# Talking-heads attention with a Fourier feed-forward: the output kept in SBUF, or summed in DRAM by adding DMAs

## The chip, the core and the metric

The kernel runs on one core of one Trainium2 chip. The metric is device time in microseconds (us); before the change it is 2406.89 us, the median of four runs (2404.97 to 2409.32). All data are float32. The program is written with a tile framework: pools hand out buffers ("tiles"), and the framework places the semaphore waits.

## The reference, cut to what matters

```python
# q, k, v: (8, 12, 448, 64); attention gives x: (8, 448, 768)
X = np.fft.fft(np.fft.fft(x, axis=1), axis=2)
u = x + np.real(X)
un = (u - mean(u)) / np.sqrt(var(u) + 1e-06)      # over the last axis
ch = np.maximum(un @ w_ch1, 0.0) @ w_ch2           # 768 -> 3072 -> 768
return u + ch
```

The attention mixes its twelve heads with 12x12 matrices before and after the softmax. What matters here is the last line: the result is u plus the feed-forward's output.

## The kernel before, in words

The first third of the time (to about 860 us) is attention and the Fourier mix; it leaves u in DRAM scratch. The rest is `ffn_phase`, and the change lies there alone.

**Tiles and loops.** The 3584 rows of u are cut into NTB = 7 row tiles of 512, the 3072 hidden columns into NC = 6 chunks of 512. The loop of L1079 runs over n = 0 to 41, with c, t = divmod(n, 7): all seven row tiles with chunk 0, then all seven with chunk 1, and so on. One such step is called a block here. A block calls `first(n)` (un times a chunk of w_ch1, then ReLU, the matmuls of L980) and `second(n, h)` (the result times a chunk of w_ch2, the matmuls of L1036). Both are done in a Strassen-Winograd form: seven products i in the order of L837 (0, 4, 5, 1, 6, 2, 3), on three PSUM accumulators named P, Q and R (L839). An accumulator is read after a product and goes on accumulating the next one.

**The output.** `second` makes 128x384 results, two (x = 0, 1) for each product. After each, VectorE adds the accumulator to a piece of u in SBUF (L1042): products 0 and 1 go to the quarter (0, 0) of the row tile's output, 4 and 6 to (1, 1), 5 and 2 to (0, 1), and 3 to (1, 0). So u itself becomes the output, chunk by chunk, and all seven u tiles (12 KB a partition each) stay in SBUF through all six chunks; in the last chunk SyncE's queue stores each finished piece (L1045, 56 stores). Three u tiles lie in one pool (L856), the other four in a pool opened after block 0 (L1092), when the mixing phase's memory is returned.

**What else runs in a block.** In chunk 0 the next row tile is normed and transposed (`stats`, `power`, `norm`, `turn`, `total`), its transposed pieces are stored to DRAM (L963), and u of the tile after next is loaded (`load_u`, L1086). From chunk 1 on the transposed pieces come back by loads (L1013) into a pool of eleven buffers, of which a block uses seven. At a chunk's last block the next chunk's weights are loaded (L903, L907). `wts` turns the weights of the next chunk from float64 into float32 and forms their seven combinations: GpSimd's queue loads pieces (L213) and stores results (L221), VectorE computes, and `wts.deal` puts a few of these VectorE operations after each product.

**What sets the order.** In the loop the instructions of TensorE and VectorE stand in the order of the program (L1071); those of ScalarE, GpSimd and SyncE are ordered by the framework's scheduler. Each engine and each queue works in order: an instruction that waits holds up what is behind it.

Of the kernel before, what the change touches and what calls it, by code (L numbers as in the profile page):

```python
# [10 lines left out]
F32 = mybir.dt.float32  # L11
U32 = mybir.dt.uint32
ALU = mybir.AluOpType
# [3 lines left out]
P = 128  # L17
B, NH, S, D = 8, 12, 448, 64
DM = NH * D
# [43 lines left out]
DH = DM // 2  # L63
# [7 lines left out]
TB = 512  # L71
NTB = B * S // TB
# [25 lines left out]
NC = 6  # L98
# [50 lines left out]
def _split(p: int, n: int):  # L149

    return [e for e in ((p, n - n % 16), (p + n - n % 16, n % 16)) if e[1]]
# [684 lines left out]

ORDER = (0, 4, 5, 1, 6, 2, 3)  # L837
OPENS = (0, 1, 4)
ACC = {0: "P", 5: "P", 6: "P", 3: "P", 1: "Q", 4: "R", 2: "R"}  # L839


@with_exitstack
def ffn_phase(ctx, tc, rest, ident, u_scr, u_rev, wts, ub_scr, out, fold_rest,
# [4 lines left out]
    nc = tc.nc  # L848

    def pool(name, bufs=1, **kw):  # L850
        return ctx.enter_context(
            tc.tile_pool(name=name, bufs=bufs, reuse_waits="tile", **kw))

    pst = pool("pst", 4)
    pun = pool("pun", 2)
    pu = [pool("pu")]  # L856
    pub = pool("pub", 11)
    pw1 = pool("pw1", 7)
    pw2 = pool("pw2", 7)
# [7 lines left out]
    NT2 = TB // P  # L867
# [4 lines left out]
    def ps_tile(key):  # L872

        n = taken[key] = taken[key] + 1
        more = len(pps) > 3 and key != "Q" and n % 3 == 0
        return pps[3 if more else "QPR".index(key)].tile(
            [P, 512], F32, name="ps" + key, tag="ps" + key, bufs=1 if more else 2)

    def next_part():
        if parts:  # L880
            parts.pop(0)(lambda: ppx.tile([P, 512], F32, name="ms", tag="ms"))

    us, ubs, w1, w2 = {}, {}, {}, {}
    mhalf = pst.tile([P, NT2], F32, name="mhalf", bufs=1)
    nc.gpsimd.memset(mhalf[:, :], -0.5)

    def load_u(t):
        us[t] = pu[-1].tile([P, NT2, DM], F32, name=f"u{t}", tag=f"u{t}")
        for x in range(NT2):
            p = 0  # L890
            while p < P:
                b, r = divmod(t * TB + x * P + p, S)
                k = sum(r >= e for e in ENDS)
                n = min(P - p, ENDS[k] - r)
                src = (u_rev if k % 2 else u_scr)[b]
                for p0, m in _split(p, n):
                    nc.sync.dma_start(out=us[t][p0:p0 + m, x, :],
                                      in_=src[r + p0 - p:r + p0 - p + m, :])
                p += n
# [5 lines left out]
    def load_w2(c, i):  # L905
        w2[i] = pw2.tile([P, FM, DH], F32, name="w2t", tag="w2t")
        nc.sync.dma_start(out=w2[i][:, :, :], in_=wts.w2[c][i])  # L907
# [25 lines left out]
    def norm(t, x):  # L933
        if x == 0:
            for i in (0, 6, 1, 2, 4, 5, 3):
                new_ub(t, i)
        uns[x] = pun.tile([P, DM], F32, name="un", tag="un")
        nc.scalar.activation(uns[x][:, :], us[t][:, x, :], ACTF.Identity,
                             bias=mvs[t][:, x, 2:3], scale=mvs[t][:, x, 1:2])

    def turn(t, x):
        un = uns.pop(x)
        for y in range(2):
            ps = ps_tile("Q")
            for c in range(NK):
                cc = NK * y + c
                tr = nc.tensor.transpose(ps[:, c * P:(c + 1) * P],
                                         un[:, cc * P:(cc + 1) * P], ident[:, :])
                if t == x == y == c == 0:

                    tc.keep_in_program_order(tr)

            copy = nc.vector.tensor_copy if t == 0 and y else nc.scalar.copy
            copy(out=ubs[t, UB[y, x // 2]][:, :, (x % 2) * P:(x % 2 + 1) * P],
                 in_=ps[:, :NK * P].rearrange("p (c n) -> p c n", n=P))

    def total(t, n):
        o, a, b = ((4, 6, 0), (5, 2, 4), (6, 2, 6), (3, 1, 5))[n]
        nc.vector.tensor_tensor(ubs[t, o][:, :, :], ubs[t, a][:, :, :],
                                ubs[t, b][:, :, :], op=ALU.subtract)  # L960
        if n == 3:
            for i in ORDER:
                nc.sync.dma_start(out=ub_scr[t][i], in_=ubs[t, i][:, :, :])  # L963

    def first(n):
# [7 lines left out]
        for k, i in enumerate(ORDER):  # L973
            if i in OPENS:
                ps[ACC[i]] = ps_tile(ACC[i])
            p = ps[ACC[i]].rearrange("p (m t) -> p m t", m=FM)
            ub = ubs.pop((n, i))
            for m in range(FM):
                for kc in range(NK):
                    nc.tensor.matmul(p[:, m, :], w1[i][:, kc, m * P:(m + 1) * P],  # L980
                                     ub[:, kc, :],
                                     start=i in OPENS and m == kc == 0,
                                     stop=kc == NK - 1, skip_group_check=True)
# [36 lines left out]
    def second(n, h):  # L1020
        c, t = divmod(n, NTB)
        h11, h12, h22, hs3, hs1, hs2 = (h[:, x] for x in range(6))
        lhs = (h11, h12, h12, h22, hs1, hs2, hs3)
        u = us[t]
        norms = c == 0 and t + 1 < NTB
        if norms:
            norm(t + 1, 0)
            norm(t + 1, 1)
        ps = {}
        for k, i in enumerate(ORDER):  # L1030
            for x in range(NT2 // 2):
                if i in OPENS:
                    ps[ACC[i], x] = ps_tile(ACC[i])
                p = ps[ACC[i], x][:, :DH]
                for kf in range(FM):
                    nc.tensor.matmul(p, lhs[i][:, kf, x * P:(x + 1) * P],  # L1036
                                     w2[i][:, kf, :], start=i in OPENS and kf == 0,
                                     stop=kf == FM - 1, skip_group_check=True)
                for r, d in {0: [(0, 0)], 1: [(0, 0)], 4: [(1, 1)], 5: [(0, 1)],
                             2: [(0, 1)], 6: [(1, 1)], 3: [(1, 0)]}[i]:  # L1040
                    us_ = u[:, 2 * r + x, d * DH:(d + 1) * DH]
                    nc.vector.tensor_tensor(us_, us_, p, op=ALU.add)  # L1042
                    if c == NC - 1 and i in (1, 6, 2, 3):
                        r0 = t * TB + (2 * r + x) * P
                        nc.sync.dma_start(out=out[r0:r0 + P, d * DH:(d + 1) * DH],  # L1045
                                          in_=us_)
            if i == 1:
                nc.vector.tensor_tensor(h12, h12, hs2, op=ALU.subtract)
            if norms and k < NT2:
                turn(t + 1, k)  # L1050
                if k + 2 < NT2:
                    norm(t + 1, k + 2)
            if norms and k >= NT2 - 1:
                total(t + 1, k - NT2 + 1)
            if n == 0:
                next_part()
            wts.deal(2 if norms and k >= NT2 else 4)
            if t == NTB - 1 and c + 1 < NC:
                load_w2(c + 1, i)

    for t in range(2):
        load_u(t)
# [8 lines left out]
    with tc.manual_schedule(engines={ET.PE, ET.DVE}):  # L1071
        for x in range(NT2):
            norm(0, x)
            turn(0, x)
        for i in ORDER:
            load_w2(0, i)
        for n in range(4):
            total(0, n)
        for n in range(NC * NTB):  # L1079
            c, t = divmod(n, NTB)  # L1080

            if c + 1 < NC and 0 <= t - (c == 0) < NK + FM:
                wts.add(c + 1, t - (c == 0))
            wts.deal(0)
            if c == 0 and t + 2 < NTB:
                load_u(t + 2)  # L1086
            second(n, first(n))
            wts.deal(1000)
            if n == 0:
                assert not parts  # L1090
                rest.close()
                pu.append(pool("pu2", side="right"))  # L1092
                beside.close()
                pps.append(pool("ppy", space=bass.MemoryType.PSUM))

# [60 lines left out]
```

## Time and profile before

| what | value |
|---|---|
| median of four runs | 2406.89 us (2404.97 to 2409.32) |
| the profiled execution: time, span | 2413.36 us, 2411.6 us |
| granted TensorE clock, mean | 0.994 |
| blocks of chunk 0 with the next tile's norm: start to start | 39.9 us (905.70, 945.57, 985.43, 1025.30, 1065.16) |
| later blocks: start to start | 36.19 us (2118.35, 2154.54) |
| busy VectorE in a block of 36 us: with weight work, without | 25.2 us, 12.4 us |
| busy ScalarE in a block of 36 us after chunk 0 | 4.24 us |
| VectorE's add of L1042, 128x384 from PSUM | 0.552 us, x588 in all |
| SyncE's issue of an output store (L1045) | 0.332 us |

A row of the profile's groups names line, engine, operation, the tiles written and read, the shape and the count; then the busy time, the mean of one in ns, the idle time of the engine ahead of them and what ended it. The rows of stretches ("windows") give the busy time of each engine in a stretch, the number of instructions, the granted clock (1.00 is full), the share of the 16 DMA engines' time that was used, and GB/s. Queues: "SPq" is SyncE's queue and "POOLq" GpSimd's.

### The profile page before, as it was taken

How to read it: one execution, taken by the hardware profiler on the slowest of the kernel's cores; microseconds unless marked ns; L12 is line 12 of the kernel's file. 1: busy time of each engine (PE TensorE's matmuls, PEld its weight loads, DVE VectorE, ACT ScalarE, POOL GpSimd, SP SyncE). 2: the span in 40 equal slices, each digit the busy share in tenths (PEclk: the TensorE clock that was granted, in tenths of full speed). 3: DMA queues.
4: the chain of work that ended last, by engine and by line, in shares of the span. 5: the costliest groups of instructions: out<-in, count | busy, mean ns of one | idle time of the engine just before them, and what ended most of it. 6: DMA issues, size and time to landing. Idle time of an engine off the chain costs nothing.

```text
span 2411.6 us, 54664 instructions
## 1 busy us (share of the span) xinstructions
PE 2362.3 (98%) x21680; PEld 1593.8 (66%) x21680; DVE 1544.6 (64%) x3139; ACT 797.7 (33%) x2055; POOL 785.0 (33%) x1255
## 2 busy tenths in 40 slices
PE   6999999999999999999999999999999999999999
PEld 2555555555555577677777777777777777777776
DVE  3888988888887757775667356635664457533333
ACT  4777767666667532221111111111111111111110
POOL 3587876968776541121111011101110011000000
PEclk9999999999999999999999999999999999999999
DMA  7565555655554566436444444534442644353331
GB/s 159 164 184 167 182 175 163 191 160 173 174 167 158 162 234 196 145 125 243 141 144 141 156 145 126 161 130 154 146 156 92 200 134 141 121 170 112 118 118 53
DMA packets 169100, 372.50 MB, mean 154 GB/s; under 512 B 36750, under 2 KB 90790, under 8 KB 168846
## 3 DMA queue, kind: packets, MB, share of 16 engines
q1 hardware_dynamic: 129902, 261.60, 33.0%
q0 software_dynamic: 33376, 106.03, 15.1%
q8 instruction: 173, 2.83, 0.5%
q10 hardware_dynamic: 5568, 1.38, 0.4%
q14 instruction: 81, 0.66, 0.1%
HBM read 211.98 MB, written 74.34 MB: 119 GB/s over the span
## 4 chain that ended last, share of the span: by engine, by line
PE 90%; DMA 4%; DVE 2%; SPq 1%; ACT 1%; issue 1%; POOL 0%; ACTq 0%; DVEq 0%; POOLq 0%
PE psP L980 18%; PE psP L1036 18%; PE psR L980 9%; PE psR L1036 9%; PE mx L486 6%; PE ms L547 5%; PE ms L459 5%; PE po L520 5%; PE psQ L1036 5%; PE psQ L980 5%; DMA Kr<-Sb 3%; PE ms L661 2%; PE ms L434 1%; SPq L475 1%; PE ms L645 1%; PE ms L580 1%
## 5 line engine op out<-in xcount | busy, mean ns | idle before, releaser
L980 PE MATMUL psP<-ub,w1t 128*128 128x256 f32 x2016 | 462.5, 379 | 0.0
L1036 PE MATMUL psP<-w2t,h 128*128 128x384 f32 x1344 | 460.9, 486 | 0.0
L980 PEld LDWEIGHTS psP<-ub,w1t 128*128 128x128 f32 x2016 | 382.8, 190 | 60.7
L213 POOL DMA_DIRECT2D raw<-in_moe_w_ch_dram x120 | 68.5, 570 | 919.3 <-DVE tmp L257 908.7
L1036 PEld LDWEIGHTS psP<-w2t,h 128*128 128x128 f32 x1344 | 254.4, 190 | 165.9
L510 POOL TENSOR_SCALAR PP<-PP,rcp 128x448 f32<-128x448 f32 x384 | 252.8, 668 | 231.4 <-DVE rcp L508 203.0
L500 ACT ACTIVATE PP<-mx,nmx 128x448 f32<-128x448 f32 x384 | 240.3, 631 | 174.2 <-DVE nmx L493 161.4
L493 DVE TENSOR_REDUCE nmx<-mx 128x1 f32<-128x448 f32 x384 | 222.5, 616 | 95.5 <-PE mx L486 93.6
L985 ACT COPY h<-psP 128x512 f32<-128x512 f32 x42 | 24.6, 585 | 765.1 <-PE psP L980 693.8
L1042 DVE TENSOR_TENSOR u<-u,psP 128x384 f32<-128x384 f32 x336 | 183.4, 552 | 141.5 <-PE psP L1036 139.3
L486 PE MATMUL mx<-Kr,kw 60*32 60x448 f32 x3072 | 233.9, 552 | 20.1 <-DMA Kr<-Sb 14.8
L980 PE MATMUL psR<-ub,w1t 128*128 128x256 f32 x1008 | 231.3, 379 | 0.0
L1036 PE MATMUL psR<-w2t,h 128*128 128x384 f32 x672 | 230.5, 486 | 0.0
L991 DVE TENSOR_TENSOR h<-h,psQ 128x512 f32<-128x512 f32 x42 | 28.9, 688 | 298.9 <-PE psQ L980 298.8
L531 DVE STREAM_TRANSPOSE Pv<-po 128x896 f32<-128x896 f32 x192 | 212.4, 1106 | 8.3 <-PE po L520 5.3
L520 PE MATMUL po<-PP,kw 60*32 60x448 f32 x3072 | 213.7, 543 | 3.0 <-DVE rcp L507 2.2
L459 PE MATMUL ms<-kT,qT 64*32 64x448 f32 (+1 forms) x3072 | 206.4, 547 | 7.5 <-ACT qT L330 6.6
L980 PEld LDWEIGHTS psR<-ub,w1t 128*128 128x128 f32 x1008 | 191.4, 190 | 25.9
L330 ACT COPY Sb<-ms 124x448 f32<-124x448 f32 x384 | 183.7, 541 | 34.6 <-DMA Kr<-Sb 16.0
L547 PEld LDWEIGHTS ms<-Pv,vv 64*64 64x64 f32 x5376 | 145.3, 134 | 70.1 <-issue 36.9
L1036 PEld LDWEIGHTS psR<-w2t,h 128*128 128x128 f32 x672 | 127.2, 190 | 87.5
L547 PE MATMUL ms<-Pv,vv 64*64 64x120 f32 x5376 | 168.3, 270 | 0.8 <-issue 0.7
(95 smaller groups left out, 2812.0 us busy)
## 6 DMA issues: line engine op xcount, KB each, us to landing
ub<-ub SPq DMA_DIRECT2D x294, 384.0 KB
Kr<-Sb SPq DMA_DIRECT2D x768, 105.0 KB
raw<-in_moe_w_ch_dram POOLq DMA_DIRECT2D x72, 256.0 KB, 3.7
raw<-in_moe_w_ch_dram POOLq DMA_DIRECT2D x48, 384.0 KB, 3.7
w<-wst POOLq DMA_DIRECT2D x126, 128.0 KB, 3.1
w<-wst POOLq DMA_DIRECT2D x84, 192.0 KB, 2.4
w1t<-w SPq DMA_DIRECT2D x42, 384.0 KB
w2t<-w SPq DMA_DIRECT2D x42, 384.0 KB
```

What stands on the lines that cost most here:

```text
L330: (nc.scalar.copy if eng == "a" else nc.vector.tensor_copy)(out=out, in_=in_)
L459: nc.tensor.matmul(pss[x][o:o + hi - lo, :S], st["qT", xx][64 * x:64 * x + 64, y, lo:hi], st["kT", xx][64 * x:64 * x + 64, y, :], start=Tr ...
L486: nc.tensor.matmul(mx[x][64 * z + o:64 * z + o + 32, :S], kw1[64 * x:64 * x + KR, o:o + 32], Kr[64 * x:64 * x + KR, z, :], start=True, sto ...
L493: nc.vector.tensor_reduce(nmx[:, :], steps[T]["mx"][x][:, :S], axis=AX.X, op=ALU.max, negate=True)
L500: nc.scalar.activation(steps[T]["PP"][:, x, :], steps[T]["mx"][x][:, :S], ACTF.Exp, bias=steps[T]["nmx", x][:, :], accum_out=steps[T]["den ...
L510: nc.gpsimd.tensor_scalar(PP[:, x, :], PP[:, x, :], rcp[:, x:x + 1], 1.0, op0=ALU.mult, op1=ALU.mult)
L520: nc.tensor.matmul(po[o:o + 32, z, :S], kw2[64 * z:64 * z + KR, y, :], PP[64 * z:64 * z + KR, :, c * HS:(c + 1) * HS], start=True, stop=True)
L531: nc.vector.transpose(g["Pv"][:, T % GT, :].rearrange("p (z s) -> p z s", z=2), steps[T]["po"][:, :, :S])
L547: nc.tensor.matmul(pss[y][64 * x:64 * x + 64, :nu * R], st["v", pr][64 * y:64 * y + 64, x, jb * D:(jb + 1) * D], _ap(Pv, 64 * y * rp + 32 ...
L980: nc.tensor.matmul(p[:, m, :], w1[i][:, kc, m * P:(m + 1) * P], ub[:, kc, :], start=i in OPENS and m == kc == 0, stop=kc == NK - 1, skip_g ...
L1036: nc.tensor.matmul(p, lhs[i][:, kf, x * P:(x + 1) * P], w2[i][:, kf, :], start=i in OPENS and kf == 0, stop=kf == FM - 1, skip_group_check ...
L1042: nc.vector.tensor_tensor(us_, us_, p, op=ALU.add)
```

## The change

u tiles live in a pool of three buffers, so a tile's buffer is used again three tiles later. In chunk 0 the adds of L1042 stay, and the finished pieces are stored to the output in DRAM at once (56 stores in blocks 0 to 6 in place of 35 to 41). From chunk 1 on, a block opens four small tiles `od` of 128x2x384 (3 KB a partition, from a pool of six buffers): ScalarE copies the first result of a quarter into it (products 0, 4, 5, 3), VectorE adds the second (products 1, 6, 2), and when the second half (x = 1) is in, GpSimd's queue issues one DMA of 384 KB that adds the tile to the output in DRAM (`accum_op=ALU.add`). Quarter (1, 0) has one product and no VectorE add.

```diff
+DEST = {0: (0, 0), 1: (0, 0), 4: (1, 1), 5: (0, 1), 2: (0, 1), 6: (1, 1), 3: (1, 0)}
...
-    pu = [pool("pu")]
+    pu = pool("pu", 3)
...
+    pd = []
+    acc = {(t, r, d): out[t * TB + 2 * r * P:t * TB + (2 * r + 2) * P,
+                          d * DH:(d + 1) * DH].rearrange("(x p) f -> p x f", p=P)
+           for t in range(NTB) for r in range(2) for d in range(2)}
...
-        us[t] = pu[-1].tile([P, NT2, DM], F32, name=f"u{t}", tag=f"u{t}")
+        us[t] = pu.tile([P, NT2, DM], F32, name="u", tag="u")
...
-        u = us[t]
+        u = us[t] if c == 0 else None
+        os = {}
...
-                for r, d in {0: [(0, 0)], 1: [(0, 0)], 4: [(1, 1)], 5: [(0, 1)],
-                             2: [(0, 1)], 6: [(1, 1)], 3: [(1, 0)]}[i]:
+                r, d = DEST[i]
+                last = i in (1, 6, 2, 3)
+                if c == 0:
                     us_ = u[:, 2 * r + x, d * DH:(d + 1) * DH]
                     nc.vector.tensor_tensor(us_, us_, p, op=ALU.add)
-                    if c == NC - 1 and i in (1, 6, 2, 3):
+                    if last:
                         r0 = t * TB + (2 * r + x) * P
-                        nc.sync.dma_start(out=out[r0:r0 + P, d * DH:(d + 1) * DH],
-                                          in_=us_)
+                        nc.sync.dma_start(out=acc[t, r, d][:, x, :], in_=us_)
+                    continue
+                if (r, d) not in os:
+                    os[r, d] = pd[0].tile([P, 2, DH], F32, name="od", tag="od")
+                o = os[r, d][:, x, :]
+                if i in (0, 4, 5, 3):
+                    nc.scalar.copy(out=o, in_=p)
+                else:
+                    nc.vector.tensor_tensor(o, o, p, op=ALU.add)
+                if last and x == 1:
+                    nc.gpsimd.dma_start(out=acc[t, r, d], in_=os[r, d][:, :, :],
+                                        accum_op=ALU.add)
...
-                pu.append(pool("pu2", side="right"))
+                pd.append(pool("pd", 6, side="right"))
```

## The prediction, as it was put on record

> **What bounds the kernel now.** I read the page's shares first, then the chain of work that ended last, then what TensorE waited for, then stretches of one block each, and last the order of events at the end.
>
> ```profile
> PE 2362.3 (98%) x21680; PEld 1593.8 (66%) x21680; DVE 1544.6 (64%) x3139; ACT 797.7 (33%) x2055; POOL 785.0 (33%) x1255
> ...
> PE 90%; DMA 4%; DVE 2%; SPq 1%; ACT 1%; issue 1%; POOL 0%; ACTq 0%; DVEq 0%; POOLq 0%
> ```
>
> TensorE has 98% of the span and 90% of the chain. A share alone can mislead, so I asked for everything TensorE waited on from 1105 us (block 6, the last of chunk 0) to the end: the answer holds no row at all. In the blocks the change rewrites, no matmul waits for anybody.
>
> ```profile
> 1105.00:1141.00 36.00, 36.00 (x141) 26.51 (x140) 14.60 (x26) 4.24 (x7) 1.07 (x2) 1.00 0.84 298
> 1249.00:1285.00 36.00, 36.00 (x140) 26.42 (x140) 25.21 (x54) 4.25 (x7) 6.01 (x11) 1.00 0.52 159
> 1358.00:1394.00 36.00, 36.00 (x141) 26.51 (x140) 12.39 (x21) 4.24 (x7) 0.00 (x0) 1.00 0.62 212
> 2262.00:2298.00 36.00, 36.00 (x140) 26.42 (x140) 12.40 (x21) 4.24 (x7) 0.00 (x0) 1.00 0.37 121
> ```
>
> The columns are stretch, length, busy us of TensorE, its weight loads, VectorE, ScalarE and GpSimd with counts, clock, DMA share, GB/s. The reader is to see that TensorE is full in all four (140 or 141 matmuls), whether VectorE has 25.2 us of work or 12.4. So VectorE's work, which the change cuts, is not what sets a block.
>
> **The change, part by part.**
>
> *VectorE and ScalarE, 35 blocks from chunk 1 on.* Before, VectorE makes 7 x 2 adds of 0.552 us a block, 7.7 us. After, it makes 3 x 2 = 6, 3.3 us, so 4.4 us a block or 155 us in all go. ScalarE gets 4 x 2 = 8 copies of 128x384 from PSUM; the nearest row is the copy of L954, the same shape, at 0.480 us: 3.8 us a block, so ScalarE goes from 4.24 to 8.1 of 36 us. Both lie beside TensorE's 36.19 us. An accumulator must be read before its next product: product 0's x = 0 half is read while its x = 1 half and product 4 run, 1.29 + 2.58 = 3.9 us, for a copy of 0.48 us. What waits there: behind a ScalarE copy only the next copy and, 2.6 us later, the next block's copy of L985. On TensorE: 0. The bound on a gain comes from the rows above: 140 matmuls in 36.00 us with much VectorE work and with little, so a block can differ by no more than one matmul, 0.26 us; over 35 blocks at most 9 us, and I take 0.
>
> *GpSimd's queue.* 4 x 35 = 140 adding DMAs. The rows of L221 and L213 give 0.55 us of GpSimd for one issue: 2.2 us a block on top of 6.0 of 36. Each waits for the last copy or add of its quarter. Behind it stand the weight loads and stores of L213 and L221; all are paced by the same products, so a wait here is about one product, 2.6 us. A weight load stands two pieces (14 VectorE operations, about four products, 10 us) ahead of its use, and a store's buffer is next written 28 VectorE operations later. Cost 0; the cover ends only if an adding DMA held the queue for 10 us.
>
> *The ring of six od tiles.* A tile opened at a block's first product takes the buffer of the quarter that was finished by the sixth of the seven products in the block before: 2.6 us (the seventh) + 18.1 us (`first`) until it is wanted, plus 1.3 us of matmul. The second tile has 18.1 + 2.6 + 1.3 = 22 us too. An adding DMA must take over 22 us to stop a copy, and through PSUM the matmuls.
>
> *What the adding DMAs take of the DMA engines.* No row shows one. Below: the output stores are packets of 1536 bytes, 66 ns each in the trace's packet records; 256 of them over 16 engines are 1.06 us. A copy reads once and writes once; an addition also reads its destination, so I take twice, 2.1 us, or 8.5 us a block: the share rises from 0.46 (the mean of a chunk's seven blocks) to 0.70. Above: of GpSimd's packets of 6144 bytes, weight loads that read DRAM beside other traffic, the slowest tenth take 0.87 us or more; 256 of these would be 14 us. I stay near the lower row, since its packets have the same size and the same target. The point from which it decides: the engines are free for 0.54 x 36.19 = 19.5 us a block, so 4.9 us a DMA, 4.6 times the plain packet. The loads of w1, w2 and of ub that share the engines are issued half a block (18 us) or a block ahead.
> The Trainium skill weighs on this too: Collectives: The Full Stack, section "The bandwidth ceiling: the fold count and why AG ≠ RS ≠ AR", says that an addition in the DMA engines is slow not for the arithmetic but for its second read, and gives half the rate of a copy. By it the DMA would be an estimated 2.1 us, as above; no run so far shows it.
>
> *Chunk 0.* The 56 stores move from the last chunk to blocks 0 to 6: 8 x 0.332 = 2.7 us of SyncE a block, each behind a VectorE add that ends 0.6 us after its matmuls. Behind them in SyncE's queue stand the stores of L963 and the loads of u. New is that u of tile t+2 waits until tile t-1 is stored: about 3 us into block t; then some 13 loads of about 0.4 us, 5 us, and 3 us to land, 11 us into the block. Its first reader (L922) stands in block t+1, 36 to 40 us after the start of block t. 25 us of cover: 0. In block 6 the DMA share is 0.84; 8 stores of 128 packets of 66 ns add 8.4/16 each, 4.2 us, 0.12, to 0.96, in the second half where the weight loads thin out. I take 0, at most 3 us (one SyncE store's landing of 2 us and a product's wait).
>
> *The end.* This is the one place where something of the change stands in the chain.
>
> ```profile
> 2404.78 4.20 SPq L1045 DMA_DIRECT2D out_dram<-u  x4
> 2404.97 2.45 PEld L1036 LDWEIGHTS psP<-w2t,h 128*128 128x128 f32 x8
> 2405.28 2.74 PE L1036 MATMUL psP<-w2t,h 128*128 128x384 f32 x8
> ...
> 2406.78 0.55 DVE L1042 TENSOR_TENSOR u<-u,psP 128x384 f32<-128x384 f32 x1 [0.73 <-PE psP L1036]
> 2408.07 0.55 DVE L1042 TENSOR_TENSOR u<-u,psP 128x384 f32<-128x384 f32 x1 [0.74 <-PE psP L1036]
> ```
>
> Before: last matmul, an add of 0.55 us to 2408.62, a 192 KB store by SyncE, whose packets run from 2409.48 to 2410.15 and whose landing ends SyncE's wait at 2410.59, then 0.97 us of closing barriers to 2411.56. So 1.97 us from issue to landing. After: a copy of 0.480 us (0.07 less) and one 384 KB adding DMA from GpSimd, the x = 0 half going only with the x = 1 half.
>
> ```profile
> raw<-in_moe_w_ch_dram POOLq DMA_DIRECT2D x48, 384.0 KB, 3.7
> w<-wst POOLq DMA_DIRECT2D x84, 192.0 KB, 2.4
> v<-X,rows POOLq DMA_INDIRECT x16, 5.3
> ```
>
> These are GpSimd's own times from issue to landing. Lower end: 2.4, a store to DRAM of half the size. Nearest: 3.7, the same 384 KB, but plain and 128 packets. Upper end: 3.7 twice, a read of the destination ahead of the write, 7.4. I take 3.7 plus the extra 1.06 us of a second read, 4.8: 4.8 - 1.97 - 0.07 = **+2.7 us** (from +0.4 to +5.4).
> The skill speaks against this queue: SBUF — State Buffer, section "Summary: rules for kernel authors", says to issue from ScalarE's or SyncE's queue where VectorE runs in its fast modes, since GpSimd's descriptor writing is then starved. At the end VectorE has nothing to run, so by it nothing is added there; in the blocks it would lengthen a DMA that has 22 us.
>
> **Sum.** 0 + 0 + 0 + 2.7: the profiled execution would go from a span of 2411.6 to 2414.3 and from 2413.36 to 2416.1 us. That execution lies 6.5 us above the median of the runs, so on the median: 2406.9 + 2.7 = **2409.6 us**, 0.11% more. A difference under 0.2% (4.8 us) can hardly be told from none for this kernel.
>
> **The rivals.**
> *Slower: the adding DMAs fill the DMA engines.* Place: every block from chunk 1 on. From 4.9 us a DMA it decides. At six times the plain packet, 6.4 us, four are 25.4 us against 19.5 free: +5.9 us x 35 = 207 us, 2614 us. For it: no row shows an adding DMA, and a chunk's last block is at 0.62 already. Against: it needs far more than the second read. 8%.
> *Slower: SyncE's queue in chunk 0.* If the stores hold up u so that norm is late in the four blocks whose u waits for a buffer, by 5 us each: +20 + 2.7, 2430 us. Against: 25 us of cover. 9%, part of it too small to tell.
> *Faster: VectorE's relief.* At most the 9 us above, 2406.9 - 9 + 2.7 = 2401 us. For it: a fifth of VectorE's feed-forward work goes. Against: TensorE waits for nobody there. 8%.
> *It does nothing at all*, the end included (landing as fast as before): 2407. That is the low end of my case.
>
> **Chances.** My case 75%: 60 within 0.2%, 14 slower by more (an end beyond +4.8, up to +5.4, or with the 3 us of chunk 0), 1 faster. DMA engines 8%, all slower. Chunk 0 9%: 7 slower, 2 within. VectorE's relief 8%: 6 faster, 2 within. Sum: faster 7, within 64, slower 29. The range goes from 2404 (the end free and half of VectorE's gain, with the runs' own spread) to 2420 (end +5.4, chunk 0 +3, and up to 5 us of a late queue); outside lie the full DMA engines, most of a late chunk 0 and a full VectorE gain.
>
> **What would show it.** Right: blocks of 36.19 us after chunk 0, no TensorE wait from 1105 us on, VectorE 4.4 us a block lighter, ScalarE at 8.1, DMA share near 0.7, and a last adding DMA that lands about 4.8 us after its issue. Wrong: TensorE waits on psP or psR for ScalarE's copies (od tiles not free), a DMA share near 1, blocks of chunk 0 longer than 39.9 us, or an end longer by more than 5.4 us.

## The result, and the profile after

The changed kernel takes 2410.26 us (median of 49 runs, 2404.46 to 2422.32) against 2405.33 us (75 runs, 2397.08 to 2414.49) for the kernel before: a ratio of 1.0024, 95% interval 1.0017 to 1.0031, so 0.24% or some 5.8 us slower. The runs of both spread by over 10 us. Part of that can be seen in the traces: the mixing phase, whose engines' order the change does not touch, hands over to the first block of the feed-forward at 856.6 us in the profiled execution before, at 852.9 us in the one after, and anywhere from 844.8 to 859.0 us in the ten profiled executions of this study. Therefore I compare stretches from there on, and not spans (2411.6 and 2413.0 us).

The page's shares of the changed kernel, the groups of its two new operations, and the issues of GpSimd's queue:

```profile
PE 2361.0 (98%) x21680; PEld 1591.3 (66%) x21680; DVE 1406.1 (58%) x2859; ACT 932.2 (39%) x2335; POOL 960.2 (40%) x1395
...
L1062 POOL DMA_DIRECT2D out_dram<-od x140 | 170.9, 1221 | 590.5 <-DVE od L1060 467.7
...
L1058 ACT COPY od<-psP 128x384 f32<-128x384 f32 x210 | 100.6, 479 | 437.1 <-PE psP L1042 437.1
...
out_dram<-od POOLq DMA_DIRECT2D x140, 384.0 KB, 6.0
```

VectorE lost 138 us of work (280 instructions fewer) and ScalarE gained 134. GpSimd spends 1.22 us on an adding DMA, which lands (its semaphore tells that the data have arrived) 6.0 us after its issue, in the median. The same stretches as before, in the changed kernel:

```profile
1105.00:1141.00 36.00, 36.00 (x141) 26.44 (x140) 14.95 (x29) 4.25 (x7) 0.37 (x1) 1.00 0.97 340
...
1249.00:1285.00 36.00, 36.00 (x141) 26.44 (x140) 21.93 (x45) 7.96 (x15) 10.81 (x16) 1.00 0.78 202
...
1358.00:1394.00 36.00, 36.00 (x141) 26.44 (x140) 11.21 (x22) 7.89 (x16) 5.85 (x6) 1.00 0.88 259
2262.00:2298.00 36.00, 36.00 (x141) 26.44 (x140) 7.97 (x13) 8.08 (x15) 4.79 (x4) 1.00 0.57 120
```

The DMA share rose (0.52 to 0.78, 0.62 to 0.88, 0.37 to 0.57), and TensorE's column did not move. What TensorE's matmuls waited for from 860 us to the end, in the changed kernel, is all of this, the same two rows and the same times as before:

```profile
PE psQ L952 <- DVE u L1049: 1.6, 5, 0.3
PE psQ L1042 <- ACT ub L959: 1.2, 5, 0.2
```

From the start of each block's first matmul to the next, both kernels have 49.09, then five times 39.86 or 39.87, then 36.19 us thirty-five times: 41 intervals, and none differs by more than 0.01 us. So nothing was lost or won in the blocks. What is left is the end. The order of events there, in the changed kernel:

```profile
2400.91 1.19 POOL L1062 DMA_DIRECT2D out_dram<-od  x1 [2.21 <-issue]
2401.54 2.74 PE L1042 MATMUL psP<-w2t,h 128*128 128x384 f32 x8
...
2402.66 1.20 POOL L1062 DMA_DIRECT2D out_dram<-od  x1 [0.56 <-DVE od L1060]
2403.03 0.48 ACT L1058 COPY od<-psP 128x384 f32<-128x384 f32 x1 [8.55 <-PE psP L1042]
2404.32 0.48 ACT L1058 COPY od<-psP 128x384 f32<-128x384 f32 x1 [0.81 <-PE psP L1042]
2405.09 1.19 POOL L1062 DMA_DIRECT2D out_dram<-od  x1 [1.24 <-ACT od L1058]
```

The last copy ends at 2404.80, GpSimd starts to issue at 2405.09, and the span ends at 2413.01. From the trace's packet records: the packets of the last three adding DMAs form one unbroken train, without a pause between one DMA and the next, from 2402.67 to 2410.93. Step by step, in us:

```
                                      before   after   difference
start of last matmul to add or copy    0.53     0.53     0.00
add or copy                            0.55     0.48    -0.07
its end to the issue                   0.03     0.29    +0.26
issue to landing seen by SyncE         1.94     6.25    +4.31
landing to the end of the span         0.97     1.67    +0.70
sum                                    4.02     9.22    +5.20
```

+5.2 us behind the last matmul is 0.22% of the time, inside the interval of the ratio (+4.1 to +7.5 us). (The prediction's 1.97 us for the store counts the 0.03 to its issue in.) The five stretches are those of one profiled execution each; how far another one can differ is seen below, at the ring of three.

### The profile page after: what moved, and what is told of

It reads as the page before. It is cut to its first block, busy times and chain, and to the rows that moved or that the text cites. A ratio compares the mean times of both kernels' runs of the same rounds, so it can differ in the third digit from the quotient of the medians.

```text
span 2413.0 us, 55276 instructions
## 1 busy us (share of the span) xinstructions
PE 2361.0 (98%) x21680; PEld 1591.3 (66%) x21680; DVE 1406.1 (58%) x2859; ACT 932.2 (39%) x2335; POOL 960.2 (40%) x1395
## 4 chain that ended last, share of the span: by engine, by line
PE 78%; issue 11%; DMA 4%; POOL 2%; DVE 2%; ACT 1%; SPq 1%; ACTq 0%; POOLq 0%; DVEq 0%
PE psP L985 15%; PE psP L1042 14%; PE psR L985 7%; PE psR L1042 7%; PE mx L486 6%; PE ms L459 5%; PE ms L547 5%; PE po L520 5%; PE psQ L1042 4%; PE psQ L985 4%; DMA Kr<-Sb 3%; POOL out_dram L1062 2%; PE ms L661 2%; PE ms L434 1%; PE ms L645 1%
## 5 line engine op out<-in xcount | busy, mean ns | idle before, releaser
L1042 PE MATMUL psP<-w2t,h 128*128 128x384 f32 x1344 | 460.9, 486 | 0.0
L1062 POOL DMA_DIRECT2D out_dram<-od x140 | 170.9, 1221 | 590.5 <-DVE od L1060 467.7
L1042 PEld LDWEIGHTS psP<-w2t,h 128*128 128x128 f32 x1344 | 254.4, 190 | 165.9
L1058 ACT COPY od<-psP 128x384 f32<-128x384 f32 x210 | 100.6, 479 | 437.1 <-PE psP L1042 437.1
L1042 PE MATMUL psR<-w2t,h 128*128 128x384 f32 x672 | 230.5, 486 | 0.0
L1042 PEld LDWEIGHTS psR<-w2t,h 128*128 128x128 f32 x672 | 127.2, 190 | 87.4
```

The lines of the kernel that those rows point to most:

```text
L1042: nc.tensor.matmul(p, lhs[i][:, kf, x * P:(x + 1) * P], w2[i][:, kf, :], start=i in OPENS and kf == 0, stop=kf == FM - 1, skip_group_check ...
L1062: nc.gpsimd.dma_start(out=acc[t, r, d], in_=os[r, d][:, :, :], accum_op=ALU.add)
```

## The experiments

The theory: the whole loss lies behind the last matmul, since the last block's adding DMAs cost more than plain stores. The rivals: the stores of chunk 0 or the adding traffic cost time in the blocks; or there is no real loss, only the spread of the runs. Ratios are to the kernel before, run beside it on one chip. "End" is the stretch from the start of the last matmul to the end of the span: 4.02 us before, 9.22 after.

**The end put back.** In the last block alone the tiles are read back and stored as before.

```diff
+        end = n == NC * NTB - 1
+        if end:
+            for r, d in ((0, 0), (1, 1), (0, 1), (1, 0)):
+                os[r, d] = pd[0].tile([P, 2, DH], F32, name="od", tag="od")
+                nc.sync.dma_start(out=os[r, d][:, :, :], in_=acc[t, r, d])
...
-                if i in (0, 4, 5, 3):
+                if i in (0, 4, 5, 3) and not end:
...
-                if last and x == 1:
+                if last and end:
+                    nc.sync.dma_start(out=acc[t, r, d][:, x, :], in_=o)
+                elif last and x == 1:
```

> The changed kernel, but in the last block (row tile 6, last chunk) the four od tiles are loaded from the output in DRAM ahead of its matmuls, VectorE adds all products to them and SyncE stores each half plainly, as the kernel before did at its end. All other 136 adding DMAs and the early stores of chunk 0 stay. Theory (the loss lies behind the last matmul alone): the stretch from the start of the last matmul to the end of the span falls from 9.2 us back to 4.0 us, blocks stay at 36.19 and 39.87 us, and the ratio to the kernel before is 1.000 (0.999 to 1.001). Rival one (the early stores or the adding traffic cost time in the blocks): at least half of the loss stays, ratio 1.0012 or more. Rival two (nothing real, the spread of the runs): ratio as for the changed kernel or anything within 0.999 to 1.003, with the end unchanged in its effect.

Measured: ratio 1.0001 (0.9983 to 1.0019), end 4.18 us. The order of events at its end:

```profile
2398.44 2.91 SPq L1067 DMA_DIRECT2D out_dram<-od  x3
...
2400.44 0.55 DVE L1065 TENSOR_TENSOR od<-od,psP 128x384 f32<-128x384 f32 x1 [0.73 <-PE psP L1047]
```

VectorE's add and SyncE's store stand there again, the span ends at 2404.1 us, 3.1 us after that add. Blocks are as in both kernels. So 136 adding DMAs and the early stores cost nothing; only the last four did. The first rival falls by these blocks and this end; the interval of the ratio alone would leave room for half of the loss (1.0012).

**The end alone.** The kernel before, with the adding path in its last block only. Row tile 6 is stored after the fifth chunk, and its own u tile serves as the four od tiles.

```diff
+                    if n == NC * NTB - 1:
+                        if i in (0, 4, 5, 3):
+                            nc.scalar.copy(out=us_, in_=p)
+                        else:
+                            nc.vector.tensor_tensor(us_, us_, p, op=ALU.add)
+                        if i in (1, 6, 2, 3) and x == 1:
...
+                            nc.gpsimd.dma_start(
...
+                                accum_op=ALU.add)
+                        continue
                     nc.vector.tensor_tensor(us_, us_, p, op=ALU.add)
-                    if c == NC - 1 and i in (1, 6, 2, 3):
+                    if c == NC - 1 - (t == NTB - 1) and i in (1, 6, 2, 3):
```

> The kernel before (u kept in SBUF, VectorE's adds, no stores in chunk 0), but row tile 6 is stored after the fifth chunk, and in the last block its products go by ScalarE's copies and four adding DMAs of 384 KB from GpSimd. Theory: this part alone brings the whole loss, 9.2 us behind the start of the last matmul in place of 4.0, ratio 1.002 (1.0015 to 1.003). Rival one (blocks): ratio 1.000, since no block has other traffic. If the four DMAs run one into the next on the DMA engines as in the changed kernel, their packets form one stretch of some 11 us that ends after the last issue by more than one DMA's own time.

Measured: ratio 1.0020 (1.0006 to 1.0034), end 10.16 us, blocks unchanged. Four DMAs of 140 bring the whole loss, so "only the spread" falls too. Their packets are one train from 2399.36 to 2410.12. The last two issues:

```profile
2402.66 1.19 POOL L1049 DMA_DIRECT2D out_dram<-u  x1 [1.35 <-DVE u L1046]
2405.09 1.22 POOL L1049 DMA_DIRECT2D out_dram<-u  x1 [1.23 <-ACT u L1044]
```

The last DMA lands 5.47 us after its issue, 0.8 us sooner than in the changed kernel. The end is 0.9 us longer all the same, because GpSimd's closing drain (the last long row of GpSimd in the trace) ends 3.0 us after the last packet; in the other kernels whose last DMAs are GpSimd's it is 0.8 to 2.2 us. What sets that is open.

**Halves.** The last block's four adding DMAs are cut into eight.

```diff
+                if last and n == NC * NTB - 1:
+                    nc.gpsimd.dma_start(out=acc[t, r, d][:, x, :], in_=o,
+                                        accum_op=ALU.add)
-                if last and x == 1:
+                elif last and x == 1:
```

> The changed kernel, with the last block's four adding DMAs cut into eight of 192 KB, each issued when its half is ready. If the end is set by how fast the adding packets run (four DMAs of 2.9 us back to back), the train of packets starts 1.3 us earlier and is otherwise as long, and the last issue is shorter by some 0.6 us: the stretch behind the last matmul's start goes from 9.2 to between 7.4 and 8.0 us. If instead a fixed time per DMA sets it, whatever its size, it stays between 8.6 and 9.2 us. If issuing is the limit (eight issues of 1.2 us), it grows over 9.2.

Measured: ratio 1.0019 (1.0002 to 1.0037), end 7.83 us. The events of GpSimd's queue:

```profile
2397.42 0.89 POOL L1062 DMA_DIRECT2D out_dram<-od  x1 [26.09 <-DVE od L1060]
2398.73 0.84 POOL L1062 DMA_DIRECT2D out_dram<-od  x1 [0.42 <-DVE od L1060]
...
2405.02 0.85 POOL L1062 DMA_DIRECT2D out_dram<-od  x1 [0.29 <-ACT od L1058]
2406.68 0.85 POOL L1062 DMA_DIRECT2D out_dram<-od  x1 [0.81 <-ACT od L1058]
```

An issue of half the rows takes 0.85 us, not 0.6. The 1024 packets run without a gap from 2398.87 to 2411.13, that is from 6.15 us ahead of the last matmul's start to 6.11 us behind it; in the changed kernel they run from 4.5 us ahead to 7.14 us behind. A start 1.6 us earlier brought the last packet 1.0 us forward; the other 0.4 us of the shorter end lie behind the last packet (1.7 us in place of 2.1). This agrees with an end that is set by the rate of the adding packets, and 7.83 us lies outside what a fixed time per DMA would give. But it is one profiled execution, and the ring of three (below), whose last block is not cut into halves, ended at 8.35 us: so 0.9 of the 1.4 us may be no more than the difference between two executions. The ratio alone can't tell this from the changed kernel.

**Plain copies.** The last block's DMAs go from the same queue without the addition (row tile 6 then lacks the first five chunks).

```diff
-                                        accum_op=ALU.add)
+                                        accum_op=(ALU.bypass if n == NC * NTB - 1
+                                                  else ALU.add))
```

> The changed kernel, with the last block's four DMAs issued from GpSimd as before but as plain copies; it leaves out the sum of the first five chunks in row tile 6. Theory: with packets of 66 ns in place of 140 to 175, a DMA has 1.06 us of packets, there is no backlog, and the stretch behind the last matmul's start is 0.5 + 0.5 + 0.3 + 1.8 + 1.1 + 0.4 + 1.7 = 6.2 us: 3.0 us of the 5.2 are the addition, 2.2 us are GpSimd's queue with one large DMA. If the queue alone were the price, it would stay near 9 us; if the addition alone, it would fall to 4 us.

Measured: ratio 1.0015 (0.9998 to 1.0031), end 5.85 us. GpSimd's queue:

```profile
2403.51 0.72 POOL L1062 DMA_DIRECT2D out_dram<-od  x1 [1.01 <-DVE od L1060]
2405.94 0.71 POOL L1062 DMA_DIRECT2D out_dram<-od  x1 [1.72 <-ACT od L1058]
```

A plain issue of the same tile takes 0.72 us and becomes 96 packets, most of 4608 bytes, that run 1.2 us; an adding one takes 1.2 us and becomes 256 packets of 1536 bytes that run 2.9 us. Of the loss of 5.2 us in these profiles, 3.4 go with the addition (its longer issue and its smaller packets included) and 1.8 with the large DMA from GpSimd's queue: 0.95 later landing, 0.70 more closing work, 0.26 from the result to the issue, less 0.07 for the faster copy.

**The ring of od tiles.** Three buffers in place of six, and two. The edit is the 6 of `pool("pd", 6, side="right")`; one profiled execution each.

> The changed kernel with three od buffers in place of six. The prediction gave six buffers a cover of 22 us; counted again, a tile takes the buffer of the sixth tile before it, and with four tiles a block that lies two blocks back, so six have one block (36 us) more. With three the tightest is the seventh product's tile, which takes the first quarter's buffer of the same block: its DMA is issued some 0.8 us after the fourth product and lands 6 us later, 6.9 us in all, and the copy wants it 2.58 x 2 + 1.29 = 6.5 us after the fourth product. So a copy waits up to 1 us, and TensorE, which needs that accumulator again only after the next product, waits for nothing: blocks of 36.19 us. If landing in the blocks takes longer than 9 us, blocks grow.

Measured: all blocks 36.19 us after chunk 0, TensorE waits as before; in four of the 35 blocks the seventh product's copy came late, by up to 1.9 us. The end is 8.35 us, 0.9 less than in the changed kernel, though the last block is the same and its four issues keep the same distances: the packets of the last three DMAs took 7.4 us in place of 8.3, and the last one landed after 5.38 us in place of 6.25. So the end of this block is worth +4.3 to +5.2 us, as two profiled executions show it.

> The changed kernel with two od buffers. The third product's copy (accumulator P) must wait for the DMA of the first quarter, issued 0.8 us after the fourth product, and the fifth product accumulates on the same P: TensorE stands for about 0.8 + 6.1 + 0.5 = 7.4 us there, and once more at the seventh product's tile, which waits for the second quarter's DMA, issued after the fifth product, wanted two products later, so 7.4 - 5.2 = 2.2 us more, unless the first wait has covered it. Blocks of 43.6 to 46 us after chunk 0, 35 x 7.4 = 260 us to 340 us more in all (2665 to 2750 us). If the ring never mattered, blocks stay at 36.19.

Measured: blocks from chunk 1 on 44.3 to 46.7 us, 299 us more in all, 2716 us. What TensorE waited for, and what ScalarE waited for, with two buffers:

```profile
PE psP L1042 <- ACT od L1058: 233.2, 35, 7.6
```

```profile
ACT od L1058 <- DMA out_dram<-od: 690.9, 65, 11.8
```

Once in each of the 35 blocks TensorE waits up to 7.6 us for ScalarE's copy, and that for the landing of an adding DMA. These waits are 233 of the 299 us. The rest goes with a lower granted clock (0.949 in this run), as the first product after a wait shows against the next:

```profile
1346.50 4.54 PE L1042 MATMUL psP<-w2t,h 128*128 128x384 f32 x8 [6.70 <-ACT od L1058]
1350.88 2.74 PE L1042 MATMUL psR<-w2t,h 128*128 128x384 f32 x8
```

That the sum fell into the expected range is so in part luck: the wait was 6.7 us a block in place of 7.4, and the clock was not in the sum. So this is the wait that the changed kernel could have had, and three buffers already remove it.

**Twice and three times the adding.** Each adding DMA is issued once more, or twice more, into scratch in DRAM; one profiled execution each.

```diff
+                    for q_ in dup:
+                        r0 = t * TB + 2 * r * P
+                        nc.gpsimd.dma_start(
+                            out=q_[r0:r0 + 2 * P, d * DH:(d + 1) * DH].rearrange(
+                                "(x p) f -> p x f", p=P),
+                            in_=os[r, d][:, :, :], accum_op=ALU.add)
```

> The changed kernel, with every adding DMA issued a second time into a scratch tensor in DRAM (its content is not used). The prediction put the point from which the DMA engines decide at 4.9 us of engine time a block's DMA, 19.5 us a block. By packets of 140 ns eight adding DMAs are 8 x 2.24 = 17.9 us: under the point, blocks stay at 36.19 us, DMA share near 0.95, and only the end grows (two more DMAs of 2.9 us a product pace: 12 us or so more). By the 175 ns seen at the end they are 22.4 us: over it by 2.9 us, blocks of up to 39 us, some 100 us in all.

Measured: every block 36.19 us; the end 16.49 us. Two blocks of chunk 1 (t = 3 and t = 6), DMA share in the last column but one:

```profile
1237.94:1274.13 36.19, 36.19 (x141) 26.60 (x140) 22.10 (x46) 8.08 (x15) 16.06 (x21) 1.00 0.97 243
1346.52:1382.70 36.18, 36.18 (x141) 26.60 (x140) 9.59 (x18) 8.08 (x15) 9.79 (x9) 1.00 1.05 288
```

By this measure the DMA engines are full, and TensorE does not notice: its waits are the same two rows as before. (The share adds up the times of the packets; it can pass 1, since up to 26 packets, more than the 16 engines, are under way at once in the records.) The end grew by 7 us, not by 12.

> The changed kernel, with every adding DMA issued two more times into two scratch tensors (content not used): 12 x 2.24 = 26.9 us (140 ns) to 12 x 2.8 = 33.6 us (175 ns) of the DMA engines a block, against 19.5 us free. If the point is where the prediction put it, the blocks of chunks 1 to 4 grow by 7.4 to 14 us, 200 to 450 us in all, with the DMA share near 1 and TensorE waiting for loads or for od tiles. If the engines take more than I thought, blocks stay at 36.19 us and only the end grows.

Measured: blocks t = 0 to 4 of chunks 2 to 4 and t = 1 to 4 of chunk 1 grow by 4.8 to 14.9 us, 157 us over all blocks, and the end is 23.56 us (2592.6 us). Two stretches of chunk 1, then what TensorE and what VectorE waited for:

```profile
1250.00:1290.00 40.00, 37.15 (x139) 26.73 (x138) 21.04 (x45) 7.88 (x15) 20.96 (x23) 0.96 1.01 234
1290.00:1330.00 40.00, 35.31 (x129) 25.55 (x128) 22.03 (x45) 6.36 (x13) 20.31 (x22) 0.91 1.02 240
```

```profile
PE psR L1042 <- DVE h L1071: 109.9, 19, 12.6
```

```profile
DVE tmp L235 <- DMA raw<-in_moe_w_ch_dram: 204.1, 19, 18.2
```

The DMA share is at 1.0, and the wait runs through the weights: a weight load stands in GpSimd's queue behind the adding DMAs and lands 11.7 us after its issue in the median (3.7 in the changed kernel), VectorE waits for it up to 18.2 us with its next product behind it, and TensorE waits for VectorE. TensorE's waits are 110 of the 157 us; a lower clock after them, as with two buffers, goes with the rest. It costs less than the 200 to 450 us I expected: the last two blocks of a chunk have no weight work and the last chunk has none at all, and none of these blocks grew, while the end grew by 14 us. What gives out first is not separated by this run: the DMA engines' time, or GpSimd's queue, in which single issues of adding DMAs now took up to 5 us.

## Why the prediction was right or wrong

*What bounds the kernel: right.* No block changed by more than 0.01 us, with VectorE 4.4 us lighter in a block without weight work (12.40 to 7.97) and ScalarE at 8.1 of 36 us, as worked out. Over all blocks VectorE lost 138 us, not the 155 forecast; in the blocks with weight work it was less than 4.4 us, and why was not followed. The rival of VectorE's relief is dead: a lighter engine that nobody waits for gave nothing.

*Chunk 0: right.* Intervals of 39.86 and 39.87 us with the early stores, and a DMA share of 0.97 in block 6 where 0.96 was forecast.

*The DMA engines' share: near, but priced by the wrong figure.* Packets of an adding DMA take 140 ns (median) against 66 for the plain stores, 2.1 times; but some take far longer, and the mean, which counts for the engines' time, is 174 ns, 2.6 times: 2.8 us a DMA where 2.1 were forecast. The share is 0.73 as the mean of chunk 1's seven blocks, where 0.70 was forecast. The point from which the engines decide, four DMAs of 4.9 us or 19.5 us a block, is not contradicted: adding twice, 18 to 20 us a block by the packet records, left the blocks alone, and three times, 24 to 30 us, did not. The Trainium skill's Collectives: The Full Stack, section "The bandwidth ceiling: the fold count and why AG ≠ RS ≠ AR", which says that an addition costs the rate of a second read, agrees with the median, 2.1 times; the mean of 2.6 is more than that, and here the measurement decides. At the end of the kernel a whole adding DMA ran 2.9 us, 2.4 times the 1.2 us of the plain one, which also had fewer and larger packets.

*GpSimd's queue: the issue was mis-sized.* 1.22 us, not 0.55: my rows were plain DMAs of 128 rows. In the blocks it cost nothing. Beside VectorE's weight work an issue took 1.23 to 1.24 us in the median, in the last chunk 1.20: the lengthening that the prediction allowed for in the blocks hardly shows. That the weight loads were the weak point of that queue was right, as three times the adding shows.

*The ring: a slip in counting.* With four tiles a block and six buffers, a tile takes the buffer of the sixth before it. For the two tiles that the prediction counted, this lies two blocks back and not one, so their cover was not 22 us but one block, 36 us, more. The tightest is a block's third tile, which takes the first quarter's buffer of the block before: 7.7 + 18.1 + 5.2 + 1.3, about 32 us. Three buffers still hold, two do not.

*The end: right in place, half in size.* This is the term that failed: +2.7 us put down, +5.2 measured, just inside its bound of +5.4 (+4.3 in the ring of three). Issue to landing was taken as 4.8 us and is 6.25. The first of the last four DMAs, with nothing ahead of it, was issued at 2397.50 and had its last packet at 2402.16; a landing comes 0.4 us behind the last packet, so 5.1 us alone. (With two od buffers the last DMA of the kernel ran alone, and landed 5.22 us after its issue.) The other 1.2 us are the backlog: a product comes every 2.58 us, an adding DMA runs 2.75 to 2.9 us, so the last one stands behind its predecessors. The second of the four was also issued late, 3.41 us after the first in place of 2.58; the profile names nothing that it waited for. The backlog is the least steady part: the last landing took 5.47 us with the end alone and 5.38 with the ring of three, so 0.3 to 0.4 us of it. I had priced one DMA by itself, and taken 2.1 us of engine time for it. The rest was not in my sum at all: 0.26 us more from the result to the issue, and 0.70 us more of closing work after the landing.
The Trainium skill's DMA: Bandwidth & Descriptors, section "Specifications", gives about 1 us to the first byte from GpSimd and 0.6 us from SyncE. Here it was 1.76 us from the issue of an adding DMA to its first packet, 1.3 us for the plain one from the same queue, and 0.83 us for SyncE's store; for this kernel the measurement decides.

*The chances.* "Within 0.2%" had 64% and the ratio came out at 0.24% (interval 0.17 to 0.31%), an end at the top of its range; that case had 14%. The mechanism was the forecast one. That the time, 2410.3 against 2409.6 us, fits so closely is luck: the kernel before came out at 2405.3 us over 75 runs, where the forecast started from 2406.9 over four, and this made up for an end that was priced too low.

## What to carry to other kernels

Work that moved between engines beside a full TensorE was worth nothing by itself; look for the one place where the moved work stands in the chain, here the last few microseconds. There, price the whole way and not the transfer alone: the result to the issue, the issue to the landing of a lone DMA (5.1 us here, against 1.94 for the plain store of half the size), the closing work, and the train of the last ones, since the backlog of DMAs that take longer than the work that feeds them is paid at the end (0.3 to 1.2 us here). And an adding DMA was fine for the many blocks with cover, while the last block was better finished with a read back and plain stores, which took the ratio from 1.0024 to 1.0001 (0.9983 to 1.0019); no version here beat the kernel before.

## What the runs showed of the hardware that was not expected

- The DMA engines at a share of 0.97 to 1.05 for whole blocks cost TensorE nothing (each adding DMA issued twice), though the slowest weight load landed only after 19.0 us; VectorE waited for such loads 8 times, at most 1.4 us.
- An adding DMA of 256 rows of 1536 bytes costs GpSimd 1.2 us to issue, the plain one 0.72 us; the plain one became mostly packets of 4608 bytes, the adding one kept 1536.
- GpSimd's closing drain ended 0.8 to 3.0 us after the last packet of its queue; which of these a kernel gets stayed open.
- After a wait of 6.7 us the next eight matmuls of TensorE took 4.54 us in place of 2.74 (two od buffers): a wait cost more than its own length.
